# A new way to a top-80 threshold, and a new order behind it, in an FFT-filter and mixture-of-experts kernel

## The chip, the cores and the metric

The kernel runs on one core of one Trainium2 chip. The core has five engines that work side by side and wait for each other by semaphores: TensorE (PE: matrix products; its weight loads are listed apart as PEld), VectorE (DVE), ScalarE (ACT), GpSimd (POOL) and SyncE (SP), which issues transfers. Transfers (DMA) of all queues share 16 DMA engines. PE writes to PSUM, a small memory that DVE and ACT read; everything else lies in SBUF or in the large memory outside the core. The metric is the device time of one execution in microseconds (us), lower is better, given as a median of several runs.

## What is computed

The reference has two parts. The first filters each of 8 sequences of 2496 rows and 256 channels in the frequency domain. The second is a mixture of 8 experts: every row goes to the expert with its greatest logit, each expert keeps only the 80 rows with the greatest gate, and all other rows of the output are zero.

```python
X = np.fft.rfft(x, axis=1)                              # x: (8, 2496, 256)
Y = X * (filt_r + 1j * filt_i)[None]
x = np.fft.irfft(Y, n=2496, axis=1).reshape(19968, 256)
logits = x @ w_gate                                     # 8 experts
expert_idx = np.argmax(logits, axis=1)
probs = np.exp(logits - logits.max(-1, keepdims=True))
probs /= probs.sum(-1, keepdims=True) + 1e-09
gate_w = probs[np.arange(N), expert_idx]
for e in range(E):
    tok_idx = np.where(expert_idx == e)[0]
    if len(tok_idx) > capacity:                         # capacity = 80
        keep = np.argpartition(-gate_w[tok_idx], capacity)[:capacity]
        tok_idx = tok_idx[keep]
    h = np.maximum(x[tok_idx] @ w1[e], 0.0)
    out[tok_idx] = gate_w[tok_idx, None] * (h @ w2[e])
```

## The kernel before

The transform of length 2496 is split as 39 times 64. For each sequence b the kernel goes through ten steps u. A step multiplies by the first table (L307), transposes (L321), multiplies by the second table (L332), multiplies by the filter on DVE (L340) and adds real and imaginary parts on POOL (L346). Then it turns the spectrum back and, in the same matmul, multiplies it by the gate weights (L355). ACT copies the spectrum out of PSUM (L367) and DVE copies the gate part (L371) and adds its second half (L375). The spectrum is written to memory (`yf`). An inverse transform of the gate part alone (`logits`, L385 and L395) gives all logits without the filtered rows.

Only the 640 kept rows are then transformed back. So the kernel must know which rows are kept before it can go on, and that decision is the subject here. It has these pieces:

- `gating(p, part)` for each pair p of sequences: greatest logit, exponentials, first position of the greatest (`first`, `fm`), gate, and `key`, which holds the gate at the chosen expert and zero elsewhere. Part 4 transposes `key` on PE and copies it to `kt` on ACT: each of the 128 lanes now belongs to one expert and one of 16 groups of rows. Part 5 takes the 8 greatest values of each lane and sequence (`cand`), their places (`cidx`) and a number that codes them (`code`).
- `pick_edge`, `pick_all`, `pick_top`, `pick_least`, `pick_tau`: the 16 greatest of each lane are spread and brought together for each expert by a matmul (`pall`, 8 partitions by 256). Ten rounds of MAX8 and MATCH_REPLACE8 give the 80th value, the threshold `tau`, and a matmul sends it back to the lanes.
- `pick_kept`, `pick_sums`, `pick_codes`, `pick_fields`, `pick_rows`: which candidates are kept, their places by running sums (matmuls), their codes sorted, unpacked into fields, and turned by one-hot matrices (`bhot`, `bval`, `bplc`) and 16 matmuls into the indices `idxb` of the rows of each sequence.
- `pick_full`, `pick_bad`: checks; if one fails, a general path (under `tc.If(n_bad > 0)`) computes everything again.
- `pick_slots`: the list of each expert, by one-hot matrices (`eplc`, `eval`) and 16 matmuls; then token numbers, and a small matrix `last` for rows of the last sequence.

All this is done twice. Round 0 takes a safe lower threshold from six sequences and settles the rows of sequences 0 to 2 (NE = 3) while the last steps u still run; the dictionary `early` says at which step v each piece is put in. Round 1 is final.

The rows are computed from tables gathered by `idxb` (`fetch`, L470, on POOL's queue): `turn_rows` transposes four tables on PE (L487) and ACT copies them (L491); `add_rows` multiplies them by the spectrum of the sequence (L498, `yb`, loaded by SP at L478). A list `work` holds these steps in alternation, a transposing one ("t") and an adding one ("m"), five of each for each of eight sequences. `go(n)` takes the next n of the list. The pieces of round 1 stand between calls of `go`, written by hand, and every engine executes its instructions in the order of the program. So `go(8)` behind `pick_top` gives PE eight steps to do while DVE does the ten rounds. Finished rows are written to `y_sel` (L508); the experts gather from it (L1040), then turn (L1056), multiply by the first weights (L1070), by the second (L1085) and scatter the result (L1090). The weights are loaded behind the spectra of the last sequences.

Of the kernel before, what the change touches and what calls it, by code (L numbers as in the profile page):

```python
# [81 lines left out]
def kernel(  # L82
# [51 lines left out]
    PB = 32768  # L134
# [5 lines left out]
    rev = consts.tile([128, E], F32, name="rev")  # L140
    nc.vector.tensor_scalar(out=rev[:], in0=iota[:, 0:E], scalar1=-1.0, scalar2=float(E),
                            op0=AL.mult, op1=AL.add)
# [6 lines left out]
    for b in range(B):  # L149
        nc.vector.tensor_scalar(out=cbase[:, b, :], in0=iota[:, 0:KC], scalar1=float(PB),  # L150
                                scalar2=4096.0 * b + 1.0, op0=AL.mult, op1=AL.add)
# [58 lines left out]
    viol = consts.tile([128, 6], F32, name="viol")  # L210
# [22 lines left out]
    with ExitStack() as actx:  # L233
# [116 lines left out]
        def turn(b, u):  # L350
            yt = st.pop(("yt", b, u))
            ps = yps.tile([128, 2, 512], F32, name=f"py_{b}_{u}", tag="y")
            for i in range(2):
                for cb in range(NDB):
                    nc.tensor.matmul(  # L355
                        out=ps[:, i, ZW * cb:ZW * cb + ZW], rhs=gi[:, cb, :],
                        lhsT=yt[:, 2 * cb + i].rearrange("p r q -> p (r q)"),
                        start=True, stop=True)
            if b < NY:
                if u == 0:  # L360
                    ysb[b] = ypool.tile([128, NS, C], F32, name=f"ys_{b}", tag="ys")
                dst = ysb[b][:, 2 * u:2 * u + 2, :]
            else:
                if u % 2 == 0:
                    st["ys"] = fspool.tile([128, SG, C], F32, name=f"ysp_{b}_{u}", tag="fs")
                dst = st["ys"][:, 2 * (u % 2):2 * (u % 2) + 2, :]
            nc.scalar.copy(out=dst, in_=ps[:, :, E:E + C])  # L367
            if u % 2 == 1:
                src = st["ys"] if b >= NY else ysb[b][:, 2 * u - 2:2 * u + 2, :]
                nc.scalar.dma_start(out=yf[b][:, 2 * u - 2:2 * u + 2, :], in_=src)  # L370
            nc.vector.tensor_copy(  # L371
                out=zs[b % 2][:, :, 2 * u:2 * u + 2].rearrange("p e s -> p s e"),
                in_=ps[:, :, 0:E])
            zz = zs[b % 2][:, :, 2 * u:2 * u + 2].rearrange("p e s -> p s e")
            nc.vector.tensor_tensor(out=zz, in0=zz, in1=ps[:, :, E + C:E + C + E], op=AL.add)  # L375
# [26 lines left out]
        def gating(p, part):  # L402
# [18 lines left out]
            elif part == 1:  # L421
                st["first"] = big("first")
                nc.vector.scalar_tensor_tensor(
                    out=st["first"][:], in0=st["sh"][:], scalar=0.0,
                    in1=rev[:].unsqueeze(1).to_broadcast([128, N1, E]),
                    op0=AL.is_equal, op1=AL.mult)
                st["fm"] = row("fm")
                nc.vector.tensor_reduce(out=st["fm"][:], in_=st["first"][:], axis=AX.X,
                                        op=AL.max)
# [7 lines left out]
            elif part == 3:  # L437
                oh = st["sh"]
                nc.vector.tensor_tensor(out=oh[:], in0=st["first"][:], in1=bc(st["fm"][:]),
                                        op=AL.is_equal)  # L440
                nc.vector.tensor_tensor(out=key[:, 0:N1, :], in0=oh[:],
                                        in1=bc(st["gw"][:]), op=AL.mult)
                nc.gpsimd.dma_start(
                    out=bass.AP(tensor=gates_dram.tensor,
                                offset=gates_dram.offset + 2 * p * S,
                                ap=[[N1, 128], [1, N1]]),
                    in_=st["gw"][:])
            elif part == 4:
                pk = pkps.tile([128, 4, 2, N2], F32, name=f"pk_{p}", tag="k")
                for i in range(3):  # L450
                    nc.tensor.transpose(pk[:, i].rearrange("p h n -> p (h n)"),
                                        key[:, 16 * i:16 * i + 16, :], ident[:])
                nc.scalar.copy(out=kt[:, :, :, 0:3].rearrange("p h n c -> p c h n"),
                               in_=pk[:, 0:3])
            else:
                for i in range(2):
                    b = 2 * p + i
                    k = kt[:, i].rearrange("p n c -> p (n c)")
                    nc.vector.max(out=cand[:, b, :], in_=k)
                    nc.vector.max_index(out=cidx[:, b, :], in_max=cand[:, b, :], in_values=k)  # L460
                nc.vector.scalar_tensor_tensor(
                    out=code[:, 2 * p:2 * p + 2, :], in0=cidx[:, 2 * p:2 * p + 2, :],
                    scalar=16.0, in1=cbase[:, 2 * p:2 * p + 2, :], op0=AL.mult, op1=AL.add)
# [49 lines left out]
        def pick_edge(rnd, nb, kr, sign):  # L513
            src = cand[:, 0:nb, :].rearrange("p b k -> p (b k)")
            row = pt([128, KR], F32, "row", rnd)
# [14 lines left out]
        def pick_all(rnd, kr):  # L530
            st["pk"] = pkps.tile([128, 512], F32, name=f"pall_{rnd}", tag="k")
            nc.tensor.matmul(st["pk"][0:E, 0:16 * kr], lhsT=ehot[:], rhs=st["sv"], start=True,
                             stop=True)
# [17 lines left out]
        def pick_tau(rnd):  # L551
            st["misc"] = pkps.tile([128, 512], F32, name=f"misc_{rnd}", tag="k")
# [3 lines left out]
            nc.vector.tensor_copy(out=st["tau"][:], in_=st["misc"][:, 48:49])  # L556

# [45 lines left out]
        def pick_fields(rnd):  # L603
# [4 lines left out]
            for i, (sh, mask) in enumerate(((15, 1023), (12, 7), (6, 63), (0, 63))):  # L608
# [5 lines left out]
        def pick_rows(rnd, b0, nb, part):  # L614
            f_t, n = st["f_t"], nb - b0
            if part == 0:
                bhot = pt([128, KR, B], F32, "bhot", rnd)[:, :, b0:nb]
                nc.vector.tensor_tensor(
                    out=bhot, in0=f_t[:, 1, :].unsqueeze(2).to_broadcast([128, KR, n]),
                    in1=iota[:, b0:nb].unsqueeze(1).to_broadcast([128, KR, n]), op=AL.is_equal)  # L620
                bval = st["bval"] = pt([128, KR, 2, B - NE], BF16, "bval", rnd)[:, :, :, 0:n]
                for i in range(2):
                    nc.vector.tensor_tensor(
                        out=bval[:, :, i, :], in0=bhot,
                        in1=f_t[:, 2 + i, :].unsqueeze(2).to_broadcast([128, KR, n]), op=AL.mult)
                st["bplc"] = xpool.tile([128, KR, 128], BF16, name=f"bplc_{rnd}", tag="x")
            elif part < 5:
                k0 = 4 * part - 4
                nc.vector.tensor_tensor(
# [3 lines left out]
            elif part == 5:  # L633
                pb = st["misc"][:, 64:64 + 2 * n]
                for k in range(KR):
                    nc.tensor.matmul(pb, lhsT=st["bplc"][:, k, :],
                                     rhs=st["bval"][:, k], start=(k == 0), stop=(k == KR - 1))
# [10 lines left out]
        def pick_full(rnd, b0, nb):  # L648
            if rnd == 0:
                nc.vector.tensor_scalar(out=viol[:, 4:5], in0=st["rcnt"][:], scalar1=float(KR),  # L650
                                        scalar2=None, op0=AL.is_ge)
# [5 lines left out]
        def pick_bad():  # L657
            rcnt, poff, tau = st["rcnt"], st["poff"], st["tau"]
# [4 lines left out]
            vt = pt([128, 1], F32, "vt", 1)  # L663
            nc.vector.tensor_scalar(out=vt[:], in0=tau[:], scalar1=1e-20, scalar2=None,
                                    op0=AL.is_gt)
            nc.vector.scalar_tensor_tensor(
                out=viol[:, 3:4], in0=poff[:, 2, 1:2], scalar=float(cap), in1=vt[:],
                op0=AL.not_equal, op1=AL.mult)
            vsum = pt([128, 1], BF16, "vsum", 1)
# [9 lines left out]
        def pick_slots(part):  # L679
            f_t = st["f_t"]  # L680
            if part == 0:
# [4 lines left out]
                                        scalar2=None, op0=AL.add)  # L686
                st["eplc"] = xpool.tile([128, KR, cap], BF16, name="eplc", tag="x")
# [11 lines left out]
            else:  # L699
                pe = st["misc"][0:cap, 128:128 + 4 * E]  # L700
                for k in range(KR):
# [3 lines left out]
                es = pt([cap, 4, E], F32, "es", 1)  # L705
# [7 lines left out]
                       idxt)  # L713
                inl = pt([cap, NO], F32, "inl", 1)
# [17 lines left out]
        with tc.manual_schedule():  # L732
# [47 lines left out]
            for v in range(LEAD):  # L780
# [8 lines left out]
                     71: [lambda: pick_tau(0), lambda: pick_kept(0, 0, NE)],  # L789
# [13 lines left out]
            for v in range(B * NU + LATE):  # L803
# [24 lines left out]
                if b > 0 and b % 2 == 0:  # L828
                    if u == LATE + 1:
                        logits(b - 1, 1)  # L830
                    if b < 6 and u in (4, 5, 6, 7, 8, 9):
                        gating(b // 2 - 1, u - 4)
                    elif b == 6 and u in (4, 5):
                        gating(2, 2 * u - 8)
                        gating(2, 2 * u - 7)
                    elif b == 6 and u in (6, 7):
                        gating(2, u - 2)
                for act in early.pop(v, []):
                    act()
# [36 lines left out]

            go(1)
            logits(B - 1, 0)
            go(1)
# [3 lines left out]
            go(4)  # L883
# [5 lines left out]
            fp = pool("fp", 2)  # L889
            spectrum(2)  # L890
            go(3)
            pick_edge(1, B, KR, 1.0)
            pick_all(1, KR)
            ntop = -(-cap // 8)
            for i in range(ntop):
                pick_top(1, i, ntop, 16 * KR)
            go(8)
            fetch(2)
            pick_least(1, cap - 1, 1.0)
            pick_tau(1)  # L900
            pick_kept(1, 0, B)
            go(1)
            pick_sums(1, NE, B)
            pick_codes(1, NE, B)
            pick_full(1, NE, B)
            pick_bad()
# [5 lines left out]
            go(2)  # L912
# [4 lines left out]
            go(1)  # L917
            pick_slots(2)
            go(next(i for i, w in enumerate(work) if w[1] == NE))
# [105 lines left out]
class Experts:  # L1025
# [20 lines left out]
    def turn(self, e):  # L1046
# [13 lines left out]
        xs = self.fp.tile([128, NDB, cap], F32, name=f"xs{nm}_{e}", tag="xs", bufs=3)  # L1060
# [433 lines left out]
```

## Time and profile before

| what | us |
|---|---|
| median of 3 runs | 494.59 (494.34 to 498.18) |
| profiled execution, its own time | 492.98 |
| span of that profile | 491.1 |
| PE busy | 451.3 (92% of the span) |
| DVE busy | 202.7 (41%) |
| ACT busy | 221.7 (45%) |
| POOL busy | 176.4 (36%) |
| DMA | 112.79 MB, 230 GB/s over the span |
| granted clock of PE, mean | 0.946 |

The times in the profile are in us from the start of its span. A row of the timeline has start, length, engine, line of the program, operation, what is written from what, the shape and the count; in brackets the idle time of the engine before it and who ended it. The granted clock is the share of its full speed that PE was allowed.

The stages in time: steps u of all sequences to about 299; round 0 from 262 to 289 among them; the rows of sequences 0 to 2 from 297 to 349, with round 1 among them from 303 to 340; the rows of sequences 3 to 7 to 404; the experts from 408 to 480.

### The profile page before, as it was taken

The page shows a single profiled execution, that of the slowest core. Times are in us where ns is not written, and L with a number is a line of the kernel's source. Part 1 is how long each engine was busy: PE and PEld are TensorE (multiplying, and loading weights), DVE is VectorE, ACT ScalarE, POOL GpSimd, SP SyncE. Part 2 cuts the span into 40 slices and gives each one's busy share as a digit, 9 for nine tenths or more (in the row PEclk, how much of TensorE's full clock was granted, in tenths as well). Part 3 has the DMA queues.
Part 4 walks back from the last instruction along what each step waited for, and adds up shares of the span by engine and source line. Part 5 has one row for each costly group of instructions (what it writes and reads, how often), then busy time and mean ns, then how long its engine had stood idle before and what let it go on. Part 6 is the DMA issues. An engine that isn't in the chain of part 4 may idle for free. (4 is left out here: it accounts for less than half of the span.)

```text
span 491.1 us, 8653 instructions
## 1 busy us (share of the span) xinstructions
PE 451.3 (92%) x3382; PEld 423.1 (86%) x3382; DVE 202.7 (41%) x582; ACT 221.7 (45%) x339; POOL 176.4 (36%) x244
## 2 busy tenths in 40 slices
PE   5889999999999999999998989977999997999990
PEld 5879999999999999999998978756888877988870
DVE  2154544547845558645488984784000000101100
ACT  3866667666776667676664424310323320011110
POOL 7587344443444435444334471112061020012210
PEclk9999999999999999999999979976999995599996
DMA  7998467778778887889622239929889999065000
GB/s 216 269 276 253 148 211 246 239 252 269 249 240 251 258 262 256 255 256 372 265 85 87 91 111 331 423 76 379 331 316 375 380 381 344 0 192 194 20 17 10
DMA packets 38323, 112.79 MB, mean 230 GB/s; under 512 B 4393, under 2 KB 13923, under 8 KB 36482
## 3 DMA queue, kind: packets, MB, share of 16 engines
q1 hardware_dynamic: 27536, 75.36, 47.1%
q10 hardware_dynamic: 7330, 22.09, 11.5%
q0 software_dynamic: 3408, 14.70, 8.7%
q8 instruction: 29, 0.48, 0.4%
q14 instruction: 20, 0.16, 0.1%
HBM read 68.97 MB, written 43.20 MB: 228 GB/s over the span
## 5 line engine op out<-in xcount | busy, mean ns | idle before, releaser
L346 POOL TENSOR_TENSOR p<-p,p 128x256 f32<-128x256 f32 x160 | 114.5, 736 | 139.0 <-DVE p L340 94.0
L340 DVE TENSOR_TENSOR p<-pb,ft 128x512 f32<-128x512 f32 x160 | 102.2, 680 | 9.6 <-PE pb L332 9.5
L313 ACT COPY t<-pa 128x480 f32<-128x480 f32 x88 | 87.1, 1001 | 26.1 <-PE pa L307 26.1
L307 PE MATMUL pa<-wf_t,x 117*128 117x120 f32 x704 | 93.3, 280 | 6.1 <-DMA x<-in_x_dram 6.0
L307 PEld LDWEIGHTS pa<-wf_t,x 117*128 117x128 f32 x704 | 87.3, 197 | 6.4 <-DMA x<-in_x_dram 5.6
L355 PE MATMUL py<-gi,p 128*128 128x136 f32 x640 | 89.3, 283 | 1.6 <-POOL p L346 1.6
L332 PE MATMUL pb<-d_t,t 128*128 128x128 f32 x640 | 86.0, 278 | 0.0
L355 PEld LDWEIGHTS py<-gi,p 128*128 128x128 f32 x640 | 81.1, 193 | 2.0 <-POOL p L346 2.0
L332 PEld LDWEIGHTS pb<-d_t,t 128*128 128x128 f32 x640 | 78.9, 193 | 0.3 <-issue 0.2
L323 ACT COPY t<-pt 128x512 f32<-128x512 f32 x80 | 46.9, 586 | 68.2 <-PE pt L321 68.2
L498 PE MATMUL po<-yb,wt 128*128 128x256 f32 x240 | 59.3, 393 | 0.6 <-ACT wt L491 0.6
L371 DVE COPY z<-py 128x16 f32<-128x16 f32 x80 | 14.8, 185 | 100.1 <-ACT ysp L367 66.0
L498 PEld LDWEIGHTS po<-yb,wt 128*128 128x128 f32 x240 | 45.3, 199 | 6.2 <-ACT wt L491 0.8
L491 ACT COPY wt<-pw 128x512 f32<-128x512 f32 x40 | 23.3, 586 | 57.4 <-PE pw L487 56.9
L321 PE MATMUL pt<-ident,t 128*128 128x128 f32 x320 | 48.5, 275 | 0.3 <-DVE p L340 0.3
L367 ACT COPY ysp<-py 128x512 f32<-128x512 f32 x60 | 35.3, 589 | 9.9 <-PE py L355 9.9
L321 PEld LDWEIGHTS pt<-ident,t 128*128 128x128 f32 x320 | 38.0, 143 | 0.5 <-DVE p L340 0.5
L1070 PEld LDWEIGHTS ph<-xs,w 128*128 128x128 f32 x256 | 36.2, 227 | 1.8 <-DVE xs L1061 1.3
L1070 PE MATMUL ph<-xs,w 128*128 128x80 f32 x256 | 36.4, 311 | 0.8 <-DVE xs L1061 0.8
L1085 PE MATMUL po<-w,hT 128*80 128x256 f32 x128 | 30.3, 393 | 0.0
L1090 POOL DMA_INDIRECT out_dram<-ys,idxs x8 | 7.5, 935 | 56.3 <-ACT ys L1088 56.3
L487 PEld LDWEIGHTS pw<-ident,gts 128*128 128x128 f32 x160 | 20.4, 145 | 8.0 <-issue 3.7
(176 smaller groups left out, 331.0 us busy)
## 6 DMA issues: line engine op xcount, KB each, us to landing
out_dram<-zero_t SPq DMA_DIRECT2D x64, 312.0 KB
x<-in_x_dram SPq DMA_DIRECT2D x40, 468.0 KB
w<-in_moe_w_dram SPq DMA_DIRECT2D x16, 1024.0 KB
yf<-ysp ACTq DMA_DIRECT2D x30, 512.0 KB
yb<-yf SPq DMA_DIRECT2D x6, 2560.0 KB
yf<-ys ACTq DMA_DIRECT2D x10, 512.0 KB
x<-in_x_dram SPq DMA_DIRECT2D x8, 234.0 KB
d_t<-d_tbl SPq DMA_DIRECT2D x5, 256.0 KB
```

The costliest lines, as they stand in the source:

```text
L307: nc.tensor.matmul(out=ps[:, i, :, 2 * NS * cb:2 * NS * cb + 2 * NS], lhsT=xt[0:NJ * N1, (2 * k + i) % JC, 128 * cb:128 * cb + 128], rhs=w ...
L313: nc.scalar.copy(out=t1[:, 2 * k - h:2 * k - h + 2], in_=ps[:])
L321: nc.tensor.transpose(ps[:, i, cb, :], t1[:, a:a + 2, :].rearrange("p r n -> p (r n)"), ident[:])
L323: nc.scalar.copy(out=t2[:].rearrange("p i c -> p (i c)"), in_=ps[:].rearrange("p i c q -> p (i c q)"))
L332: nc.tensor.matmul(out=ps[:, cb, i], rhs=d_t[:, 2 * u + i, :], start=True, stop=True, lhsT=t2[:, i, 128 * cb:128 * cb + 128])
L340: nc.vector.tensor_tensor(out=pt, in0=ps[:].rearrange("p c s r q -> p (c s) r q"), in1=f.unsqueeze(2).to_broadcast([128, 2 * NDB, 2, NQ]), ...
L346: nc.gpsimd.tensor_tensor(out=yt[:, :, r, :], in0=yt[:, :, r, :], in1=pr[1][:, :, 1 - r, :], op=op)
L355: nc.tensor.matmul(out=ps[:, i, ZW * cb:ZW * cb + ZW], rhs=gi[:, cb, :], lhsT=yt[:, 2 * cb + i].rearrange("p r q -> p (r q)"), start=True, ...
L367: nc.scalar.copy(out=dst, in_=ps[:, :, E:E + C])
L498: nc.tensor.matmul(pos[t][:, 0, 0:C], lhsT=wts[t, g // 2][:, g % 2, i, :], rhs=ybs[t][:, s, :], start=(s == 0), stop=(s == NS - 1))
L1070: nc.tensor.matmul(ph[:, fc // 4, fc % 4, 0:cap], lhsT=self.w1s[e][:, k, 128 * fc:128 * fc + 128], rhs=xs[:, k, :], start=(k == 0), stop=( ...
L1085: nc.tensor.matmul(po[0:cap, :], lhsT=hT[:, fc, :], rhs=self.w2s[e][:, fc, :], start=(fc == 0), stop=(fc == NFC - 1))
```

## The change

It has six parts.

1. *Threshold.* Round 1 finds it by halving. The values of an expert are brought not to 8 partitions but to all 128 lanes (the mask `same` as float, 128 columns, instead of `ehot`), so that each lane sees the 256 values of its expert. Each lane has its own 16 values in falling order, with 2.0 ahead of them. Four times it selects one of its values, counts how many of the 256 are as great, and moves down if there are at most 80, else up. `pick_top`, `pick_least` and `pick_tau` remain for round 0.
2. *Gating.* The search for the first of equal logits goes: `key` takes the gate wherever the logit equals the greatest, and an accumulating compare counts equals in `ties`; if there are any, the general path is taken. `kt` is copied in two halves, and the eight greatest of both sequences are taken ahead of their places (a new part 6).
3. *z copies.* For the last two sequences ACT copies the gate part out of PSUM, ahead of the spectrum, instead of DVE.
4. *Codes.* A code now has the sequence in its highest bits, then the place. Sorted codes therefore put the late sequences first, and the row indices need only the first 12 (K0, K1) of 16 codes of a lane: 12 matmuls, three quarters of `bhot` and `bval`, three instead of four pieces of `bplc`. The checks are widened to match.
5. *Order.* Behind the threshold come the codes and the row indices, then the rest: `eplc` is a new part 3 of `pick_slots` behind the row indices, the checks come behind five more steps of `work`, and `diag`, `inl`, `last` are a new part 4 behind eight more. The counts of `go` change: 1, 4, 3, 8, 1, 2, 1 become 1, 4, 4, 5, 6, 5.
6. *Buffers.* `xs` in the experts has the pool's two buffers instead of three.

```diff
     KC, KR = 8, 16
-    PB = 32768
+    PB, BB = 4096, 1 << 19
+    K0 = K1 = 12
...
+            zz = zs[b % 2][:, :, 2 * u:2 * u + 2].rearrange("p e s -> p s e")
+            if b >= B - 2:
+                nc.scalar.copy(out=zz, in_=ps[:, :, 0:E])
             nc.scalar.copy(out=dst, in_=ps[:, :, E:E + C])
...
-            nc.vector.tensor_copy(
-                out=zs[b % 2][:, :, 2 * u:2 * u + 2].rearrange("p e s -> p s e"),
-                in_=ps[:, :, 0:E])
+            if b < B - 2:
+                nc.vector.tensor_copy(out=zz, in_=ps[:, :, 0:E])
             nc.vector.tensor_tensor(out=zz, in0=zz, in1=ps[:, :, E + C:E + C + E], op=AL.add)
...
             elif part == 1:
-                st["first"] = big("first")
-                nc.vector.scalar_tensor_tensor(
-                    out=st["first"][:], in0=st["sh"][:], scalar=0.0,
-                    in1=rev[:].unsqueeze(1).to_broadcast([128, N1, E]),
-                    op0=AL.is_equal, op1=AL.mult)
-                st["fm"] = row("fm")
-                nc.vector.tensor_reduce(out=st["fm"][:], in_=st["first"][:], axis=AX.X,
-                                        op=AL.max)
+                junk = gpool.tile([128, N1, E], BF16, name=f"same_{p}", tag="same")
+                nc.vector.tensor_scalar(
+                    out=junk[:], in0=st["sh"][:], scalar1=0.0, scalar2=None, op0=AL.is_equal,
+                    op1=AL.add, accum_out=ties[:, p:p + 1])
...
-                oh = st["sh"]
-                nc.vector.tensor_tensor(out=oh[:], in0=st["first"][:], in1=bc(st["fm"][:]),
-                                        op=AL.is_equal)
-                nc.vector.tensor_tensor(out=key[:, 0:N1, :], in0=oh[:],
-                                        in1=bc(st["gw"][:]), op=AL.mult)
+                nc.vector.scalar_tensor_tensor(
+                    out=key[:, 0:N1, :], in0=st["sh"][:], scalar=0.0, in1=bc(st["gw"][:]),
+                    op0=AL.is_equal, op1=AL.mult)
...
+        def pick_sorted():
+            row, t = st["row"], None
+            allv = st["pk"][:, 0:16 * KR]
+            bs = pt([128, 5, 4], F32, "bs", 1)
+            at = bs[:, 4, 3:4]
+            nc.vector.memset(at, float(KR // 2))
+            for i, s in enumerate((8, 4, 2, 1, 0)):
+                c, n, low = (bs[:, i, j:j + 1] for j in range(3))
+                sel = pt([128, B * KC], F32, "rest", f"s{s}")[:, 0:KR + 1]
+                nc.vector.scalar_tensor_tensor(
+                    out=sel, in0=iota[:, 0:KR + 1], scalar=at, in1=row[:],
+                    op0=AL.is_equal, op1=AL.mult, accum_out=c)
+                if s == 0:
+                    break
+                nc.vector.tensor_scalar(out=st["sv"], in0=allv, scalar1=c, scalar2=None,
+                                        op0=AL.is_ge, op1=AL.add, accum_out=n)
+                old, at = at, bs[:, i, 3:4]
+                nc.vector.tensor_scalar(out=low, in0=n, scalar1=float(cap), scalar2=float(s),
+                                        op0=AL.is_le, op1=AL.mult)
+                nc.vector.tensor_scalar(out=at, in0=low, scalar1=old,
+                                        scalar2=-(s / 2 if s > 1 else 1.0), op0=AL.add,
+                                        op1=AL.add)
+            st["tau"] = c
...
-            for i, (sh, mask) in enumerate(((15, 1023), (12, 7), (6, 63), (0, 63))):
+            for i, (sh, mask) in enumerate(((12, 127), (19, 7), (6, 63), (0, 63))):
...
             elif part < 5:
                 k0 = 4 * part - 4
+                if k0 >= kk:
+                    return
...
+            FG = (1, 4, 4, 5, 6, 5)
             go(1)
             logits(B - 1, 0)
-            go(1)
+            go(FG[0])
             logits(B - 1, 1)
             for part in range(4):
                 gating(NP - 1, part)
-            go(4)
+            go(FG[1])
             gating(NP - 1, 4)
             gating(NP - 1, 5)
...
+            st["same"] = t2pool.tile([128, 2, C], F32, name="same_f", tag="t2")[:, 0, 0:128]
+            nc.scalar.copy(out=st["same"], in_=same[:])
             spectrum(2)
-            go(3)
+            go(FG[2])
             pick_edge(1, B, KR, 1.0)
             pick_all(1, KR)
-            ntop = -(-cap // 8)
-            for i in range(ntop):
-                pick_top(1, i, ntop, 16 * KR)
-            go(8)
+            gating(NP - 1, 6)
+            pick_sorted()
+            go(FG[3])
             fetch(2)
-            pick_least(1, cap - 1, 1.0)
-            pick_tau(1)
+            pick_misc(1)
             pick_kept(1, 0, B)
-            go(1)
             pick_sums(1, NE, B)
             pick_codes(1, NE, B)
-            pick_full(1, NE, B)
-            pick_bad()
             pick_fields(1)
             pick_slots(1)
             for part in range(5):
                 pick_rows(1, NE, B, part)
             pick_slots(0)
-            go(2)
+            go(FG[4])
             pick_rows(1, NE, B, 5)
             pick_rows(1, NE, B, 6)
             for t in range(NE, 6):
                 fetch(t)
-            go(1)
+            pick_slots(3)
+            go(FG[5])
+            pick_full(1, NE, B)
+            pick_bad()
+            go(next(i for i, w in enumerate(work) if w[1] == NE))
             pick_slots(2)
-            go(next(i for i, w in enumerate(work) if w[1] == NE))
+            go(8)
+            pick_slots(4)
...
-        xs = self.fp.tile([128, NDB, cap], F32, name=f"xs{nm}_{e}", tag="xs", bufs=3)
+        xs = self.fp.tile([128, NDB, cap], F32, name=f"xs{nm}_{e}", tag="xs")
```

## The prediction, made before the changed kernel was run

> **What bounds the kernel now.** I read the page's 40 slices first, then the timeline of PE, then windows with the granted clock, then the timelines of DVE and POOL around each gap of PE. The chain that ended last holds only the last row write and says nothing about the middle.
>
> ```profile
> PE   5889999999999999999998989977999997999990
> DVE  2154544547845558645488984784000000101100
> PEclk9999999999999999999999979976999995599996
> DMA  7998467778778887889622239929889999065000
> ```
>
> PE is full from slice 3 to 20. It has holes in slices 21 to 23 and 26 to 27 (258 to 344 us), where DVE is busiest and the clock falls, and again near 410 us. So the kernel is TensorE work plus holes. Slices 26 and 27 are the final pick:
>
> ```profile
> 320.47 1.89 PE L498 MATMUL po<-ys,wt 128*128 128x256 f32 x8
> 322.87 0.38 PE L553 MATMUL misc<-edge,ehot_t 8*128 8x1 f32 x2 [0.51 <-DVE edge L548]
> 326.60 0.16 PE L672 MATMUL misc<-vsum,ones_bf 128*128 128x1 bf16 x1 [2.28 <-DVE vsum L671]
> 326.62 3.76 PE L498 MATMUL po<-ys,wt 128*128 128x256 f32 x8
> 339.32 0.36 PE L725 MATMUL misc<-diag,ones_bf 80*128 80x240 bf16 x1 [2.95 <-DVE diag L720]
> ```
>
> PE waits for DVE in the middle of its row work (L498), and the same eight matmuls then take 3.76 us instead of 1.89. The windows show why (columns: window and its length, then busy time of PE, PEld, DVE, ACT, POOL, then granted clock, DMA share, GB/s):
>
> ```profile
> 280.80:284.20 3.40, 1.73 (x13) 1.31 (x13) 3.37 (x6) 1.17 (x2) 1.85 (x2) 1.00 0.38 157
> 321.70:325.15 3.45, 1.87 (x14) 1.19 (x13) 2.44 (x13) 0.59 (x1) 0.00 (x0) 1.00 0.00 1
> 325.15:335.40 10.25, 8.32 (x37) 6.60 (x37) 8.12 (x32) 0.96 (x2) 3.03 (x5) 0.51 0.40 132
> 407.05:431.00 23.95, 22.28 (x95) 20.80 (x96) 1.96 (x5) 0.88 (x2) 0.95 (x1) 0.50 0.42 146
> ```
>
> A stretch of about 3.4 us with 1.6 us of idle PE was followed by half clock, twice. Once tripped, the clock stayed low for 10 us at 325 and for 24 us at 407. A hole costs more than its idle time.
>
> **The final pick, step by step.** Call one row group a pair: a transpose step (L487, 0.43 us) and an add step (L498, 1.73 us), 2.17 us together. Times below are on the clock of before.
>
> *Gating.* The first-of-equals search (L423, L428 at 0.48 each, and L439 at 0.42) goes; one accumulating compare over 312 elements comes. No such row exists. The nearest, L561 (64 elements, 0.28 plus 0.08 for reading the accumulator), scales to about 0.6. The key is ready near 307.3 instead of 308.0, so PE's 0.28 at L451 goes. The copy to kt in two halves (ACT, 0.85 for the whole) lets the first MAX8 start earlier; the index searches (1.3 us) move behind the sort row. The spread ends near 311 instead of 312.8; PE reaches the gather-all matmul at 312.4, after one transpose step more, so its 0.38 goes too. The copy of the lane mask on ACT (128 elements, under the 0.37 of L503) is hidden by ACT's idle 1.2 us.
>
> *Threshold.* Ten MAX8 and nine MATCH_REPLACE8 (0.42 + 0.08 + 0.40) took 313.58 to 322.65, and edge, broadcast matmul and tau went to 323.45: 9.9 us on DVE, against 8.7 us of PE cover. Now there are four rounds of: compare and count over 256 PSUM elements, two one-element operations, a select over 17 elements with accumulator. Compare: MAX8 goes from 0.22 (64 elements, L518) to 0.42 (256 from PSUM, L540), 0.20 more, so L561's 0.28 becomes 0.48, plus 0.08; one-element rows are 0.14 to 0.20 start to start; the select is a short row (0.17) plus 0.08. That is 1.24 a round, 5.0 for four. Ends: 3.5 if the short ones overlap as L661 and L664 do (0.07 apart), 6.5 if every accumulator read stalls its reader by 0.3. I take 5.0. The tau matmul goes. Threshold at 318.0, kept and counts (L561 to L569) at 318.7.
>
> *Cover.* PE now has three add and two transpose steps (6.1 us) behind the gather-all matmul: 312.95 to 319.0. The counts come 0.3 earlier, so no hole; with the upper end, 1.2 us of one.
>
> *Row indices first.* The places, codes, fields and one-hots (L587 to L629) are 6.0 us of DVE less one of four bplc (0.73) and a quarter of bhot and bval (0.24), so about 5.3; six steps of PE (6.5 us) cover them. The fullness and bad checks (L653 to L676, about 1.1 us, now 1.8 with the longer check) and their matmul move behind the row indices, under five more steps (4.8 us): the 2.28 hole goes. eplc (1.49) moves behind the indices too, so the 0.48 goes. In POOL's queue nothing changes places: the eval products, then gathers 3 to 5, each when its indices are there; gather 2 waits for nothing of the pick. On SP the spectrum loads keep their add steps. ACT's new z and lane-mask copies stand before copies that wait for the same matmuls, so nothing is queued behind a new wait. The slot list's last part (inl, diag, last) moves behind eight more steps: the 2.95 goes. Sum of idle removed: 0.28 + 0.38 + 0.51 + 0.24 + 2.28 + 0.48 + 2.95 = 7.1 us. Without holes, no half clock: 325.15 to 335.4 held 8.3 us of PE work at half speed (4.15 lost), 338.8 to 342.2 held 2.9 (1.45 lost): 5.6. With the tau matmul and eight short matmuls fewer, about 13.3.
>
> *Walked forward instead of subtracted*, PE's order with these prices starts the rows of sequence 3 at 335.1; before, at 349.12: 14.0. I keep 14.0. What is late next is their gather: row indices at 326.9, POOL issues it at 327.2; before, issue to full landing was 7.8 us (334.21 to about 342.0, behind a spectrum load), so 335.0. It is a tie; up to 1 us could be lost.
>
> [...]
>
> **The early pick (258 to 298 us).** Here DVE is the bound: from 259.7 to 289.3 it is busy 28.05 of 29.6 us. The z copy (L371) moves to ACT for the last two sequences: 0.21 off DVE per step, nine steps, 1.9. On ACT it is an estimate from L503 and L491 (0.37 for 256, 0.59 for 512): about 0.17, under ACT's idle. The fourth bplc of round 0 goes (1.19), bhot and bval shrink (0.12), gating gives 0.65 before it, a memset adds 0.07. The row indices (289.2) come at about 285.5. But then:
>
> ```profile
> 290.03 1.08 POOL L470 DMA_INDIRECT gts<-rows_tbl,idxb  x1 [0.15 <-issue]
> 297.56 0.66 PE L487 MATMUL pw<-ident,gts 128*128 128x128 f32 x4 [0.84 <-DMA gts<-rows_tbl,idxb]
> ```
>
> The first gather needs 7.5 us whatever DVE does, and POOL does its products first, so it would be issued at 286.4 and land at 293.9: 3.65 gained. PE, freed, runs out of work near 290 and idles about 3.2 of the 4 us before it. That is above the 1.6, so I expect a trip there: 3.4 to 6.8 us at half clock, 2 us lost. Net 1.6. Ends: +3.6 without a trip, 0 with a long one.
>
> **What stays.** The experts' entry:
>
> ```profile
> 407.89 0.69 PE L1056 MATMUL px<-ident,xg 80*128 80x80 f32 x2 [3.62 <-DMA xg<-y_sel,idxg]
> ```
>
> The write of y_sel (394.31) and the gather behind it (401.91, landing 6.2 later) crawl through queues full of weight loads. [...] Fewer xs buffers cost nothing: each is read by layer 1 of its expert before the third turn, and PE's order covers that; without the cover it is the 0.42 before L1070.
>
> **Sum.** 14.0 + 1.6 = 15.6 off the profiled execution's 492.98 (span 491.1 and 1.9 around it): 477.4. The median of the three runs, 494.59, is 1.6 above that execution; carried over, 479.0.
>
> **Rivals.**
> - *Transfers become the bound* (0.15). From 340 on the DMA share is about 1.0. The spectrum load of sequence 4 would be issued at 323.7 instead of 330.45, only 6.8 earlier, and all later transfers follow it. If PE waits for them, the late gain is 6.8, not 14.0: 486. Against it: spectra land 10 us or more before use. For it: the tie above, and the tail's gather, which waits behind weights.
> - *The experts' hole closes too* (0.07): the write of y_sel meets a thinner weight stream; 3.6 and 11 less, 464.
> - *Slower: the fallback runs* (0.04). The new check sends everything down the general path if a lane holds over 12 in round 0 or in the last five sequences, or if any token has two equal top logits. Price from rows: eight tiles of five pairs (10.85 each) and eight experts (7.1 each) are at least 144 us more: above 620. From the reference's inputs the fullest lanes hold 7 and 9; the closest two top logits differ by 1.3e-7, so a tie in the kernel's arithmetic is possible but rare; I give it a few per cent. One tie decides.
> - *The gain is eaten* (0.06): the count rounds stall PE each time and the trip of the early pick lasts as at 407; 488 to 496.
>
> **Numbers.** The likeliest case (0.68) spans 475 to 483. The range 472 to 486 adds a late gather or the missing early trip. About 1% (5 us) is what a measurement here can tell from no change. Faster 0.88, within 1% 0.07, slower 0.05.
>
> **What would show it.** Right: clock 1.00 throughout the final pick, no PE wait on vsum, diag or edge, the first rows of sequence 3 turned 14 to 17 us before 349. Early step: the first gts wait grows from 0.84 to 1 to 3 us, with half clock behind it. Wrong if PE waits on the counts for over 1 us, if gts or yb waits appear after 335, or if the half clock near the experts is gone.

## The result, and the profile after

| what | before | after |
|---|---|---|
| median, us | 495.32 (494.34 to 498.18, 4 runs) | 480.78 (479.11 to 482.70, 4 runs) |
| ratio to before | | 0.970, 95% interval 0.9659 to 0.9741 |
| profiled execution, us | 492.98 | 482.70 |
| span of that profile, us | 491.1 | 480.8 |
| DVE busy, us | 202.7 | 187.8 |
| granted clock, mean | 0.946 | 0.955 |

The change makes the kernel 3.0% faster: 14.5 us by the medians, 10.3 us between the two profiled executions (492.98 is under all four timed runs of the kernel before, 482.70 is the slowest of the four after). Three later executions, two of six of the changed kernel when it was run again and one of four of a run with 7 added matmuls, took over 1.5% longer than the fastest of the same kernel, and the medians and ratios here leave them out.

The slices of the page after (each slice is 12 us):

```profile
PE   4979999999999999999999987998999988999990
DVE  2135544445654536644447993584100000001100
PEclk9979999999999999999999999999899995599996
DMA  7986468788788788789942228879999997074000
```

The clock row shows most of it. The 7 of slice 23 and the 7 and 6 of slices 26 and 27 are gone; an 8 is left at slice 28. The two 5s at the experts are still there. New is a 7 in slice 2, near 28 us, where the change drops no more than a small setup instruction of DVE. The timeline of PE shows the pick itself:

```profile
311.55 0.60 PE L537 MATMUL pall<-spread,same_f 128*128 128x256 f32 x2
...
318.04 0.17 PE L606 MATMUL misc<-cnt,before 128*128 128x5 bf16 x1
...
324.93 0.45 PE L669 MATMUL misc<-bval,bplc 128*128 128x10 bf16 x12
...
330.04 0.17 PE L715 MATMUL misc<-vsum,ones_bf 128*128 128x1 bf16 x1
...
336.98 1.06 PE L485 MATMUL pw<-ident,gts 128*128 128x128 f32 x8 [2.62 <-DMA gts<-rows_tbl,idxb]
...
346.57 0.27 PE L773 MATMUL misc<-diag,ones_bf 80*128 80x240 bf16 x1
```

No bracket follows the counts, the indices, the checks (vsum) or diag: PE waits for none of them any more. The only long wait left in this stage is a new one, 2.62 us for the table rows of sequence 3. The windows after it (window, length, busy PE, PEld, DVE, ACT, POOL, then clock, DMA share, GB/s):

```profile
325.00:335.40 10.40, 9.36 (x74) 8.25 (x72) 4.18 (x26) 2.13 (x4) 4.03 (x3) 1.00 0.94 390
338.50:341.90 3.40, 3.40 (x10) 2.54 (x10) 0.00 (x0) 0.22 (x1) 0.00 (x0) 0.50 0.96 384
396.60:420.50 23.90, 21.97 (x95) 20.57 (x96) 1.96 (x5) 0.88 (x2) 0.94 (x1) 0.50 0.38 132
```

Full clock through the pick, then 3.4 us at half clock behind the new hole, and the 24 us at the experts as before.

**Where the 10.3 us came from.** Cut both profiles at two events, the first transposing of table rows and the transposing for sequence 3. To the first, 297.56 before and 296.74 after: 0.8 gained. Between the two, 51.6 (to 349.12) and 40.2 (to 336.98): 11.3 gained. From there to the end, 142.0 and 143.9: 1.9 lost, nearly all of it the 3.4 us at half clock. The line of the kernel before for sequence 3, and the first transposing after:

```profile
349.12 1.04 PE L487 MATMUL pw<-ident,gts 128*128 128x128 f32 x8
```

```profile
296.74 0.66 PE L485 MATMUL pw<-ident,gts 128*128 128x128 f32 x4 [1.35 <-DMA gts<-rows_tbl,idxb]
```

The first stretch gained more than it shows. In the profiled execution after, PE waited 2.80 us for DVE at 29.42 and spent 6.8 us at half clock from 27.9. So the same group of 16 first-table matmuls starts at 37.83 before and at 40.65 after, 2.8 us late. Counted from that group, the first transposing comes after 259.7 us before and after 256.1 here, 3.6 gained; the ten other profiles with the whole early part have 255.9 to 256.1. Of the 12 profiles with the change or most of it, all but two have such a stretch near 30 us and the one profile of the kernel before has none; one trace does not tell whether the change makes it more frequent.

### The profile page after: what moved, and what is told of

Read it like the earlier page. It is cut to its first block, busy times and chain, and to the rows that moved or that the text cites. A ratio compares the mean times of both kernels' runs of the same rounds, so it can differ in the third digit from the quotient of the medians.

```text
span 480.8 us, 8658 instructions
## 1 busy us (share of the span) xinstructions
PE 445.1 (93%) x3372; PEld 419.4 (87%) x3372; DVE 187.8 (39%) x560; ACT 222.2 (46%) x364; POOL 177.0 (37%) x244
## 5 line engine op out<-in xcount | busy, mean ns | idle before, releaser
L339 DVE TENSOR_TENSOR p<-pb,ft 128x512 f32<-128x512 f32 x160 | 102.2, 680 | 14.5 <-issue 6.6
L354 PE MATMUL py<-gi,p 128*128 128x136 f32 x640 | 88.0, 280 | 2.2 <-POOL p L345 2.2
L354 PEld LDWEIGHTS py<-gi,p 128*128 128x128 f32 x640 | 79.8, 190 | 2.6 <-POOL p L345 2.6
L496 PE MATMUL po<-yb,wt 128*128 128x256 f32 x240 | 58.3, 388 | 0.9 <-ACT wt L489 0.9
L496 PEld LDWEIGHTS po<-yb,wt 128*128 128x128 f32 x240 | 44.3, 194 | 6.5 <-ACT wt L489 1.3
L374 DVE COPY z<-py 128x16 f32<-128x16 f32 x60 | 11.2, 186 | 91.7 <-ACT ysp L369 57.9
L485 PE MATMUL pw<-ident,gts 128*128 128x128 f32 x160 | 24.2, 275 | 4.0 <-DMA gts<-rows_tbl,idxb 4.0
## 6 DMA issues: line engine op xcount, KB each, us to landing
x<-in_x_dram SPq DMA_DIRECT2D x40, 468.0 KB
```

Of the source, the lines that this page charges most:

```text
L339: nc.vector.tensor_tensor(out=pt, in0=ps[:].rearrange("p c s r q -> p (c s) r q"), in1=f.unsqueeze(2).to_broadcast([128, 2 * NDB, 2, NQ]), ...
L354: nc.tensor.matmul(out=ps[:, i, ZW * cb:ZW * cb + ZW], rhs=gi[:, cb, :], lhsT=yt[:, 2 * cb + i].rearrange("p r q -> p (r q)"), start=True, ...
L496: nc.tensor.matmul(pos[t][:, 0, 0:C], lhsT=wts[t, g // 2][:, g % 2, i, :], rhs=ybs[t][:, s, :], start=(s == 0), stop=(s == NS - 1))
```

## The experiments

Each run has its own runs of the kernel before on the same chip, and chips differ: the kernel before had medians of 497.54, 491.62 and 496.29 us in the three groups. So ratios are compared, and times only within a group.

| run | median, us | before, us | ratio (95%) |
|---|---|---|---|
| changed kernel, first measurement | 480.78 | 495.32 | 0.970 (0.9659 to 0.9741) |
| old order | 489.23 | 497.54 | 0.9846 (0.977 to 0.9922) |
| old threshold | 489.13 | 497.54 | 0.9844 (0.9791 to 0.9896) |
| early part undone | 484.69 | 497.54 | 0.9732 (0.9668 to 0.9795) |
| eplc later | 480.05 | 497.54 | 0.9672 (0.9615 to 0.9728) |
| spectrum later | 478.51 | 491.62 | 0.9725 (0.966 to 0.9791) |
| 7 matmuls before the experts | 465.87 | 491.62 | 0.9479 (0.9425 to 0.9534) |
| these three together | 469.17 | 491.62 | 0.9535 (0.9484 to 0.9586) |
| changed kernel again | 479.17 | 496.29 | 0.9679 (0.9624 to 0.9734) |
| spectrum in halves | 476.20 | 496.29 | 0.9614 (0.9561 to 0.9666) |
| halves, eplc later, 7 matmuls | 467.66 | 496.29 | 0.9433 (0.9388 to 0.9478) |
| halves, eplc later, 10 matmuls | 469.41 | 496.29 | 0.9477 (0.9427 to 0.9526) |

### New pieces in the old order

```diff
-            go(FG[2])                    # 4
+            go(3)
             pick_edge(1, B, KR, 1.0)
             ...
             pick_sorted()
-            go(FG[3])                    # 5
+            go(8)
...
             pick_codes(1, NE, B)
+            pick_full(1, NE, B)
+            pick_bad()
             pick_fields(1)
             ...
             pick_slots(0)
-            go(FG[4])                    # 6
+            pick_slots(3)
+            go(2)
```

The slot list's last two parts follow one step after the gathers, as they did before.

> The changed kernel with all its new pieces (bisection, gating, z copies, 12 codes), but the pieces of round 1 in the old order: 8 steps behind the bisection, checks ahead of the fields, eplc ahead of the indices, the slot list in one piece. Theory A (the order removes holes of PE, and with them the half clock): the waits on vsum (about 2.3 us), diag (3.0) and off_e (0.5) come back and with them 10 to 14 us at half clock; the 2.6 us wait for gather 3 goes. 486 to 490 us. Theory B (the shorter threshold search is what gains, the order little): 480 to 483 us.

0.9846, or 487.7 us on the scale of the first measurement, inside what theory A gave and above theory B. Its timeline has the holes back:

```profile
324.07 0.16 PE L715 MATMUL misc<-vsum,ones_bf 128*128 128x1 bf16 x1 [2.90 <-DVE vsum L714]
328.56 0.44 PE L669 MATMUL misc<-bval,bplc 128*128 128x10 bf16 x12 [2.06 <-DVE off_e L726]
335.98 0.26 PE L773 MATMUL misc<-diag,ones_bf 80*128 80x240 bf16 x1 [2.99 <-DVE diag L768]
```

With the short threshold and none of the order, about half of the gain is gone. The half clock behind these holes was 3.4 us twice in this profile (from 329.6 and 336.4), less than the 10 to 14 expected; the holes were 2.2 us larger than expected instead. That fits a cover that PE uses up faster at full clock: the eight matmuls behind vsum took 1.97 us here and 3.76 before.

### Old threshold in the new order

```diff
-            pick_sorted()
+            for i in range(ntop):
+                pick_top(1, i, ntop, 16 * KR)
             go(FG[3])
             fetch(2)
+            pick_least(1, cap - 1, 1.0)
             pick_misc(1)
+            pick_tau(1)
```

The gather-all matmul goes to 8 partitions again, and the copy of the lane mask is dropped.

> The changed kernel with the old threshold (ten MAX8, nine MATCH_REPLACE8, matmul back) in the new order. Theory A: DVE needs about 9.9 us from the gather-all matmul to the threshold where PE has 6.1 us to do, so one hole of about 4 us before the counts, and a half clock of 3.4 to 7 us behind it (2 to 3.5 lost); the other holes stay away. 485.5 to 488.5 us. Theory B (the search is the gain): 490 us or more, near the kernel before.

0.9844, or 487.6 us on the same scale: inside theory A. The hole is where the count of cover put it:

```profile
321.57 0.38 PE L577 MATMUL misc<-edge,ehot_t 8*128 8x1 f32 x2 [3.08 <-DVE edge L573]
322.77 0.17 PE L602 MATMUL misc<-cnt,before 128*128 128x5 bf16 x1 [0.83 <-DVE cnt L595]
```

3.9 us in two pieces, as expected (about 4), and 3.4 us at half clock from 322.5. By the medians, taking away either the order or the threshold costs about half of the gain; but both runs keep the early part, so what they have left is not the other's share. The traces separate it. From the first transposing to that of sequence 3 is 51.6 us before, 50.6 in the old-order run (about 1.7 of that from half clock at 295, which came by chance), 46.1 in this one and 40.2 after. There the order is worth 10.4 us with the short threshold and 5.5 with the old one; the short threshold is worth 5.9 in the new order and 1 to 3 in the old (the 5.5 and the 1 to 3 include the shorter gating and the 12 codes). So the short search brings little by itself: the order spends on the later pieces the steps of PE that the search no longer needs.

### Early part undone

```diff
-            if b >= B - 2:
-                nc.scalar.copy(out=zz, in_=ps[:, :, 0:E])
...
-            if b < B - 2:
-                nc.vector.tensor_copy(out=zz, in_=ps[:, :, 0:E])
+            nc.vector.tensor_copy(out=zz, in_=ps[:, :, 0:E])
...
-            f_t, n, kk = st["f_t"], nb - b0, K1 if rnd else K0
+            f_t, n, kk = st["f_t"], nb - b0, K1 if rnd else KR
```

> The changed kernel with the z copies of the last two sequences on DVE again and 16 codes for round 0. Theory A (DVE is the bound from 260 to 289 us and the first gather follows it): DVE gets 1.9 + 1.2 us back, the first gather of row tables is issued about 3 us later, and so is all behind it: 483 to 485 us. Rival (the gather and PE have that slack): within 0.7 us of the changed kernel, 480 to 481.5 us.

The ratio, 0.9732, does not tell 3 us from none (its interval holds 0.970). The traces do, since both profiles reach the first gather-all matmul (L534, or L531 here) at 264.4. The first gather of table rows, on POOL, after and with the part undone:

```profile
288.99 1.08 POOL L468 DMA_INDIRECT gts<-rows_tbl,idxb  x1 [0.15 <-ACT t L322]
```

```profile
291.90 1.08 POOL L465 DMA_INDIRECT gts<-rows_tbl,idxb  x1 [0.15 <-issue]
```

2.9 us later, and PE turns the rows 2.6 us later (299.37 against 296.74); 3.0 later counted from the first-table matmuls near 40 us, as above. DVE is the bound of that stage (before, busy 28.05 of the 29.60 us from 259.70) and the gather carries its gain on.

### The new hole: eplc, or the load ahead of the gather

In the profile after, gather 3 took 2.04 us to issue and gathers 4 and 5 took 0.99. DVE wrote eplc from 325.89 to 327.38, just then. Two runs tell what holds gather 3 up.

```profile
326.25 2.04 POOL L468 DMA_INDIRECT gts<-rows_tbl,idxb  x1 [3.47 <-DVE idxb L678]
```

In the first, `pick_slots(3)`, which writes eplc, stands behind `pick_bad()`:

> The changed kernel with eplc (1.49 us of DVE, two inputs from SBUF) behind the checks instead of right behind the row indices. Theory P (eplc keeps POOL from writing the descriptors of gather 3: 2.04 us for that issue, 1.0 for the others): the issue takes 1.0 us, gather 3 lands 1 us earlier, the 2.6 us hole shrinks to about 1.6 and the half clock may go: 478 to 480 us. Theory Q (gather 3 stands behind the spectrum load of sequence 4 whenever it is issued): the issue is shorter, the landing and the hole are not: 480 to 481.5 us.

```profile
325.47 1.03 POOL L468 DMA_INDIRECT gts<-rows_tbl,idxb  x1 [3.22 <-DVE idxb L678]
```

```profile
335.91 1.06 PE L485 MATMUL pw<-ident,gts 128*128 128x128 f32 x8 [2.33 <-DMA gts<-rows_tbl,idxb]
```

The issue is back to 1.03 us, and the hole is still 2.33: issue to use is 10.4 us here and 10.7 after. eplc did slow the issue, but that was not what the rows waited for; 0.9672 is within the interval of the changed kernel. This is theory Q, though the hole is 0.3 us shorter and no half clock followed it in this profile.

In the second, the 2.6 MB load of sequence 4 goes behind the gathers. SP has no wait that would hold it back, so ACT issues it:

```diff
-                        if t + 3 < B:
+                        if t + 3 < B and t != 1:
                             spectrum(t + 3)
...
             go(FG[5])
+            ybs[4] = ypool.tile([128, NS, C], F32, name="yb_4", tag="ys")
+            nc.scalar.dma_start(out=ybs[4], in_=yf[4])
             pick_full(1, NE, B)
```

> The changed kernel with the spectrum load of sequence 4 issued from ACT's queue some 8 us later (behind the copy of the last of the five steps), so behind the issue of gathers 3 to 5. Theory Q (gather 3 waits behind that load): gather 3 lands 7.5 to 8 us after its issue, about 334, the 2.6 us hole and the 3.4 us at half clock behind it go: 476 to 478 us. Rival (a gather lands some 10.7 us after issue however free the transfers are, because three are written one behind the other): hole unchanged, 480 to 482 us; or the load of sequence 4 is then late itself, and PE waits for it near 347.

```profile
330.21 1.06 PE L485 MATMUL pw<-ident,gts 128*128 128x128 f32 x8
...
344.36 0.63 PE L485 MATMUL pw<-ident,gts 128*128 128x128 f32 x4 [4.24 <-DMA gts<-rows_tbl,idxb]
```

The wait for gather 3 is gone: issued at 322.25 and ready when PE came, 8.0 us later at the most. The packets show the reason: with the load ahead, in the profile after, the gather's first packet moved 2.7 us after its issue had ended (331.03); here it moved after 0.7 us (324.99). But the load now shares the transfers with gathers 4 and 5, and gather 4 is late by 4.24 us, with a half clock behind it. Theory Q is right about the cause, and the cure only moved the wait; 0.9725 is no better than the changed kernel.

Half of the load on each side of the gathers:

```diff
-            nc.sync.dma_start(out=ybs[t], in_=yf[t])
+            n = NS // 2 if t == 4 else NS
+            nc.sync.dma_start(out=ybs[t][:, 0:n], in_=yf[t][:, 0:n, :])
...
             go(FG[5])
+            nc.scalar.dma_start(out=ybs[4][:, NS // 2:NS], in_=yf[4][:, NS // 2:NS, :])
```

> The changed kernel with the spectrum load of sequence 4 in two halves: the first when it was issued, the second from ACT's queue about 8 us later, behind the issue of gathers 3 to 5. Theory Q (gather 3 waits for the 2.6 MB ahead of it, and the whole load put behind it made gather 4 or the spectrum late): with half of it on each side the 2.6 us hole before the rows of sequence 3 goes and no hole of 4 us comes near 345: 2.5 us less than the changed kernel, 4 where that one lost the clock there. If the sum of transfers until 350 is the limit, the hole comes back near 345: within 1 us of the changed kernel.

```profile
334.39 1.07 PE L486 MATMUL pw<-ident,gts 128*128 128x128 f32 x8
335.70 1.56 PE L497 MATMUL po<-yb,wt 128*128 128x256 f32 x6 [0.24 <-ACT wt L490]
```

No wait at 334, none at 345, and full clock from there to the experts. 476.20 against 479.17 for the changed kernel on the same chip, 3.0 us less, where 2.5 to 4 were expected. The two intervals overlap (0.9561 to 0.9666 and 0.9624 to 0.9734), so the size is not sharp, but the hole is gone and no other came. The repeat of the changed kernel was for this group:

> The changed kernel itself, for the same chip as the next three. 0.97 of the kernel before, as measured.

It gave 0.9679, as before.

### Is the half clock at the experts caused by the hole?

```diff
             ex.extra = st["yr"], st["last"]
+            warm = pkps.tile([128, 512], F32, name="warm", tag="k")
+            for _ in range(7):
+                nc.tensor.matmul(warm[:, 0:C], lhsT=ident[:], rhs=w1s[0][:, 0, 0:C], start=True,
+                                 stop=True)
```

> The changed kernel with 7 matmuls (128x256, about 3 us in all, result unused) in the hole before the experts' first rows. Theory C (the half clock behind the hole is caused by the hole): the clock stays at 1.00 near 397, the first two experts run in 3.7 instead of 7.1 us each: 10 to 11 us faster than the changed kernel, 469 to 472 us. [...]

```profile
389.51 3.19 PE L985 MATMUL warm<-w,ident 128*128 128x256 f32 x14
392.59 0.42 PE L1115 MATMUL px<-ident,xg 80*128 80x80 f32 x2
...
394.09 3.80 PE L1129 MATMUL ph<-xs,w 128*128 128x80 f32 x32 [0.42 <-DVE xs L1120]
...
399.22 3.80 PE L1129 MATMUL ph<-xs,w 128*128 128x80 f32 x32 [0.44 <-DVE xs L1120]
```

The clock of this run from 395 to 415:

```profile
395.00:415.00 20.00, 19.56 (x147) 17.38 (x146) 2.19 (x6) 2.24 (x5) 2.89 (x3) 1.00 0.60 213
```

Layer 1 of the first two experts takes 3.80 us each instead of 7.12. In the profile after, the first expert's layer 1 and the first layer 2 are

```profile
400.08 7.12 PE L1125 MATMUL ph<-xs,w 128*128 128x80 f32 x32 [0.42 <-DVE xs L1116]
...
417.94 4.86 PE L1140 MATMUL po<-w,hT 128*80 128x256 f32 x16
```

Theory C holds: the 24 us at half clock came from a hole of about 3 us (3.21 in the profile after), and 3.19 us of matmuls whose result nobody reads remove it. Layer 1 with its 80 columns did not lower the clock by itself: behind the matmuls it ran at 1.00 from 395 to 415. Behind the hole it ran at 0.50: in the profile after, the half clock from 396.6 lasts through layer 1 of two experts and ends at 420.5, 2.5 us after layer 2 began. The median is 25.8 us under the kernel before of its group; the changed kernel is 14.5 under its own. That is 11.2 more, where 10 to 11 were expected.

The cure did not act every time. The fourth execution of this run took 481.0 us, as long as without the matmuls, at a mean clock of 0.956 against 0.983 to 0.990 in the other three. That fits the long stretch at half clock being back, but no trace of it was kept. The 16 executions of the three later runs with such matmuls took 465.3 to 472.1 us.

The three edits together:

> The changed kernel with eplc later, the spectrum load of sequence 4 later and the 7 matmuls before the experts. If the three act on different holes, the gains add: 465 to 469 us. If the later load makes another transfer late, or the hole before the experts grows by what the middle gains, 470 to 476 us.

0.9535, not better than the matmuls alone. Gather 3 was in time, but the spectrum of sequence 4 was late, as the second outcome had it:

```profile
348.67 1.62 PE L496 MATMUL po<-yb,wt 128*128 128x256 f32 x3 [3.69 <-DMA yb<-yf]
```

With the load in halves instead:

> The split load, eplc behind the checks, and 7 matmuls before the experts. The holes are different ones, so the gains add: 13 to 15 us less than the changed kernel, 0.94 of the kernel before. If transfers are the limit behind 340: as with the 7 matmuls alone, 0.948.

467.66 against 479.17 for the changed kernel on the same chip: 11.5 less, short of the 13 to 15 expected; ratio 0.9433 to the kernel before. It beats both kernels. What the halves and the later eplc add to the matmuls alone (0.9479) is not sharp, since the intervals overlap. In its profile the clock is full from 34 us to the last expert:

```profile
PEclk9989999999999999999999999999999999999997
```

And with 10 matmuls:

> As the last one with 10 matmuls (4.3 us) instead of 7 (3.0 us) before the experts. If the hole there is 3 to 3.5 us, PE is late by about 1 us, and the clock never falls there: 0.5 to 1 us slower in the median than with 7, with no run 10 us above the others. If 7 leave a hole that costs the clock in some runs, this one is faster in those.

469.41, 1.7 us more, of which three matmuls at 0.43 us are 1.3; the intervals overlap. In this group seven were enough: none of the six executions with 7 took over 468.0 us.

## Why the prediction was right, and where its terms were off

The forecast was 479.0 us with a range of 472 to 486; measured were 480.78. The mechanism held: PE's holes and the half clock among them were the cost, and moving PE's steps under DVE's work removed both. That the total came so close is partly luck. The late part was put at 14.0 us and gave 11.3, with 1.9 lost behind it; the early part was put at 1.6 and gave 3.6. The two errors, 4.6 and 2.0, have opposite signs. Together that is 13.0 between the profiles without the late start, and 14.5 by the medians, against 15.6.

Of the prediction's own signs of being right, the full clock through the pick and the absent waits on vsum, diag and edge came; the first rows of sequence 3 were turned 12.1 us before 349 (15.0 without the late start), and 14 to 17 were said. One of its signs of being wrong came too: a wait for gts after 335. By its steps:

- *The final pick.* The walk gave 37.5 us from the first transposing (297.56) to that of sequence 3 (335.1). Measured: 40.2, less the 2.6 of the new hole, 37.6; it is 37.2 in the four runs with the load moved or halved and 7 matmuls or none. The stretch shrank by 11.3, more than the 7.1 of idle time alone. The seven holes and the half clock among them are gone, as listed. The old-order run brought three of the holes back, the old-threshold run brought another.
- *The threshold.* A round was put at 1.24 us from scaled rows. It measured 1.24 (312.19 to 313.43 between two counts):

```profile
312.19 0.48 DVE L554 TENSOR_SCALAR_CACHE_REDUCE spread<-pall,bs 128x256 f32<-128x256 f32 x1 [0.69 <-PE pall L537]
...
313.15 0.24 DVE L549 SCALAR_TENSOR_TENSOR rest_s<-iota,bs,row 128x17 f32<-128x17 f32 x1
```

- *The tie that was lost.* The step that failed is "issue to full landing was 7.8 us" for gather 3. I had read it from the packets of the profile before, where PE came too late to show the wait. Issue to use measured 10.7, with the same load ahead of the gather in both kernels. The run with the load moved shows 8.0 at most without the 2.6 MB ahead of it. The loss was allowed as "up to 1 us"; it was 2.6, and 1.7 more at half clock. Moving the whole load only moved the wait.
- *The early pick.* 3.65 us were expected at the first transposing ahead of any trip. Measured from the same matmuls near 40 us, it is 3.6; only 0.8 is left of it in the times as they stand, because of the late start. The run with the z copies and the 16 codes undone puts their share at 3.0, against 1.9 + 1.2 + 0.1 in the sum.
- *The trip behind the early pick* was priced at 2 us. In the profile after it is absent: PE idles 1.38 and 1.35 us within 4 us (2.21 of the 3.40 from 293.30), more than the 1.6 that the forecast took from two stretches of one trace, and the clock stays at 1.00. In the old-order run and in the last one, with the same holes, 3.4 us at half clock follow, at 295: two of the eleven profiles with this early part. It is a chance, and a sum should carry it as one.
- *What stays.* The experts' hole (3.21 against 3.62) and the 23.9 us at half clock (21.97 us of PE work at 0.50, so about 11 lost) stayed; the stretch from there to the end is 83.1 us after and 83.2 before.
- *The rivals.* The transfers did not become the bound of the stage, but one of them did bind once. The fallback did not run, and the hole at the experts did not close by itself.

## What to carry to other kernels

Where PE has holes, count them twice, once as idle time and once as the half clock that may follow, and look in the trace for a hole with a long stretch at half clock behind it: there it can pay to fill it with work that nobody needs. Here 3.21 us of hole had 23.9 us at half clock behind them, and 7 matmuls took off 11.2 us more than the change alone. When a pick or a sort is made shorter, its cover is set free; most of the gain came here only when that cover was moved in front of the pieces that still wait. And before advancing a transfer, read its landing under the load it will meet, from the row of a reader that waited or of a gather just behind it, not from packet sums: here a gather behind a load of 2.6 MB took 10.7 us from issue to use, and at most 8.0 without it.

## What the runs showed of the hardware

The stretches at half clock, the idle end of the program aside, are 6.8, 10.2, 3.4 and 23.9 us long in the profile before, and 6.8, 3.4 and 23.9 in the profile after. Idle time alone does not tell when one comes. In the profile before, PE was idle for 1.67 of the 3.40 us from 280.80, and 6.8 us at half clock followed. In the profile after it was idle for 2.21 of the 3.40 us from 293.30 and the clock stayed at 1.00; it was idle for 2.12 of the 3.40 us from 335.10, and 3.4 us at half clock followed. No run tests what decides it.

At the experts the half clock lasted through layer 1 of two experts in both profiles. It ended after layer 2 had begun, by 3.0 us before (428.12 to 431.1) and by 2.5 after (417.94 to 420.5); no run tests whether layer 2 is the reason.

The issue of a gather on POOL took 2.04 us with eplc running beside it on DVE, and 1.03 with eplc moved away; why was not tested.
